# Half of V in loads of four heads, and wq issued ahead of x, in a cached-attention block

## The chip, the cores and the metric

The kernel runs on one core of one Trainium2 chip, in one launch. The metric is the device time of that core in microseconds (us): 235.49 us, the median of three runs from 235.37 to 235.5.

The engines that the text speaks of are TensorE (matrix products, PE in the profile, with its weight loads as PEld), VectorE (DVE), ScalarE (ACT), GpSimd (POOL) and SyncE (SP). SP does no arithmetic here; it issues nearly all the loads from memory.

## The reference

One decode step of a transformer block for a batch of two, all in float32. `c` gives six modulation vectors; the normalized and modulated `x` is projected to 32 query heads, which attend over the last 4096 positions of a cache with 8 key/value heads; `wo` projects back; a second normalized half is an MLP of width 1792.

```python
mod = (silu(c) @ w_mod).reshape(2, 6, 1, 512)
sa, ca, ga, sb, cb, gb = (mod[:, i] for i in range(6))
h = layernorm(x) * (1 + ca) + sa
x = x + ga * attention(h, k_cache, v_cache, wq, wo)   # window of 4096, 4 query heads per kv head
h = layernorm(x) * (1 + cb) + sb
x = x + gb * (silu(h @ w1) @ w2)
```

The cache window is most of the data: 2 batches x 8 heads x 4096 positions x 128 values, 32 MB for K and 32 MB for V. `w_mod` is 6 MB, `wq` and `wo` 8 MB each, `w1` and `w2` 3.5 MB each.

## The kernel before

**The ring.** All large loads go through `slots`, a ring of eight slots of 4096 floats per partition (`stream`, L70). `load_pair` (L77) takes two slots for the K or V of two heads of one batch (4 MB, 32 KB per partition); `load_runs` (L88) takes what a weight needs. A load waits until what stood in its slots has been read. All of these loads are issued by SP in program order, so a load that waits holds up those behind it. `w_mod` takes slots 0 to 2, `wq` slots 4 to 7.

**The start.** `w_mod`, `x` and `wq` are issued by SP (L105, L113, L114), the four small pieces of `c` by ScalarE (L109). `c` goes through the silu (`cT`, `scT`); 32 products make the modulation in `m_a` and `m_sp` (L259, L262). After those of k = 0 the program has the statistics of `x` (`moments`, L219: two small products, L227 and L235, and a square root). `h_a`, `hq_T` (L271 to L273) and the 32 products of `q` (L290) follow. Instructions outside the order kept by hand are placed by a planner, by when it thinks their inputs ready; those wrapped in `inorder` keep the program's order on their engine. `place` (L300) turns a half of `q` and copies it into `qbd`, the weights of the score products; `place(0)` stands ahead of the loop, `place(1)` in step 2.

**The loop.** There are eight steps, each for two heads of one batch. `fetch(s + 1)` issues K of the next step, then V of this one. `keys` transposes K on VectorE in eight pieces (L349), `scores` multiplies (L362), `maxima` and `exponentials` make the probabilities `pr`. `turn` (L403) transposes them (`xp`), spreads them (`zp`), runs four products (`pT`) and two ScalarE copies (L423) into `ptb`, the weights for V. `weighted` (L430) runs 16 products of 512 columns per step against V and copies the result out; `collect` (L448) adds the copy into `o_all` with four small products. In step s the loop transposes and scores K of s, and does `turn` and `weighted` of step s - 1.

**The end.** `wo`, `w1` and `w2` follow V in the ring; the projection, the MLP and the output close the kernel.

Of the kernel before, what the change touches and what calls it, by code (L numbers as in the profile page):

```python
# [23 lines left out]
def adaln_block(  # L24
# [45 lines left out]
    def stream(n=1):  # L70
# [3 lines left out]
        turn_of[0] = i + n  # L74
        return slots[:, i % RING : i % RING + n, :].rearrange("p s e -> p (s e)")

    def load_pair(cache, s):  # L77


        i, b = divmod(s, B)  # L80
        t = stream(2)
        nc.sync.dma_start(
            t,
            cache[b, 2 * i : 2 * i + 2, SK - W :, :].rearrange("e (u n) d -> u e (n d)", u=P // 2),
        )
        return t

    def load_runs(w, per, lo, hi):  # L88
# [18 lines left out]
    for b in range(B):  # L107
        for lo in (0, 2):
# [39 lines left out]
        id16[:, :, None].to_broadcast([P, 16, 2]),  # L148
        half[:, None, :].to_broadcast([P, 16, 2]),
    )  # L150
    odd = const([P, 2], "odd")
    nc.vector.tensor_reduce(
        odd, ident.rearrange("p (a r) -> p r a", r=2), axis=AX.X, op=ALU.add
# [15 lines left out]
    nc.gpsimd.tensor_copy(  # L169
        selh[:, :, 2 * HQ - 8 : 2 * HQ].rearrange("p m (e g) -> p m e g", e=2),  # L170
        id4.rearrange("p (e m g) -> p m e g", e=2, g=G),
    )

    quad = const([P, 4, P], "quad")
# [20 lines left out]
    for t in mrow:  # L195
        nc.gpsimd.memset(t, 0.0)

    ptb = [const([P, 16, 2, 16], f"ptb{i}") for i in range(2)]
# [6 lines left out]
    oTn = const([P, 32, 32], "oTn")  # L205
    nc.gpsimd.memset(oTn, 0.0)
    mod_sp = const([P, 4, P], "mod_sp")
    x1 = const([P, P], "x1")

# [124 lines left out]
    kt, vt, wot, kT = {}, {}, [], {}  # L334
    s_ps, pr, o_ps, o_sb = {}, {}, {}, {}

    def fetch(s):
# [16 lines left out]
    def scores(s, j):  # L354

        if j == 0:
            s_ps[s] = bank("A", f"s{s}")
        i, b = divmod(s, B)
        for c in range(2):
            for e in range(2):  # L360
                r, h = 64 * e + 32 * c, 2 * i + e
                inorder(nc.tensor.matmul(  # L362
                    s_ps[s][r : r + 32, :],
                    qbd[h // 4][:, h % 4, b, j, :],
                    kT[s, j][:, 32 * c : 32 * c + 32, e:32:2],
                    start=(j == 0),
                    stop=(j == 3),
                ))
# [17 lines left out]
        ))  # L386

    def exponentials(s):
        bp = bank("B", f"bp{s}")
# [4 lines left out]
        inorder(nc.scalar.activation(  # L394
            pr[s].rearrange("p t k -> p (t k)"),
            s_ps[s],
            AF.Exp,
            bias=bias,
            scale=SCALE,
            accum_out=rowsum[:, s : s + 1],  # L400
        ))

    def turn(s):  # L403

        xp = once.tile([P, 16, 32], F32, tag="xp", name=f"xp{s}")
        inorder(nc.vector.transpose(xp, pr[s]))  # L406
        zp = once.tile([P, 4, 16, 16], F32, tag="zp", name=f"zp{s}")
        inorder(nc.vector.tensor_mul(  # L408
            zp,
            xp[:, None, :, 0:16].to_broadcast([P, 4, 16, 16]),  # L410
            quarter[:, :, None, None].to_broadcast([P, 4, 16, 16]),
        ))
        tp = bank("C", f"pT{s}")[:, : 2 * P]
        for i in range(4):
            inorder(nc.tensor.matmul(  # L415
                tp[32 * i : 32 * i + 32, :],
                mix.rearrange("p v e -> p (v e)"),
                zp.rearrange("p y t x -> p (y t) x")[:, :, 4 * i : 4 * i + 4],
                start=True,
                stop=True,  # L420
            ))
        for e in range(2):
            inorder(nc.scalar.activation(  # L423
                ptb[s % 2][:, :, e, :],
                tp.rearrange("p (w z) -> p w z", z=16),
                AF.Copy,
                scale=odd[:, e : e + 1],
            ))

    def weighted(s):  # L430
# [14 lines left out]
        o_sb[s] = once.tile([P, 4 * DH], F32, tag="wide", name=f"ob{s}")  # L445
        inorder(nc.scalar.copy(o_sb[s], o_ps[s]))  # L446

    def collect(s):  # L448

        i, b = divmod(s, B)  # L450
        lo = 2 * HQ - 8 - (HQ * b + 2 * G * i)
        for m in range(4):
            r = 64 * (m % 2)
# [4 lines left out]
                start=(s == 0 and m < 2),  # L458
                stop=(s == STEPS - 1 and m >= 2),
                skip_group_check=True,  # L460
            ))
# [264 lines left out]
```

## Time and profile before

| what | value |
|---|---|
| median of the runs | 235.49 us |
| the profiled execution, span from first to last instruction | 233.6 us |
| median less span | 1.9 us |
| bytes moved by DMA | 97.68 MB, mean 418 GB/s |
| TensorE busy | 160.1 us (69%) |
| VectorE busy | 114.8 us (49%) |
| ScalarE, GpSimd busy | 28.9 us (12%), 10.5 us (5%) |
| mean granted TensorE clock | 0.927 |

In the profile, a row of the timeline has the start in us, the duration, the engine, the line of the kernel, the operation, the tiles (written <- read), their shapes and a count; at its end, in brackets, stands the idle time of the engine ahead of it and what ended that idle time. "SPq" and "ACTq" rows are issues of loads. Several instructions of one kind are merged into one row. A row of the stretches has the stretch and its length, the busy time and count of PE, PEld, DVE, ACT and POOL, the granted TensorE clock, the share of the DMA engines and GB/s. A row of DMA issues ends with the us from issue to landing. In rows of one tile's instructions stand the least, median and greatest duration in ns.

### The profile page before, as it was taken

Reading aid. Unit: us, or ns where it says so; the run is one execution under the profiler, and the core shown is the slowest. Engines: PE = TensorE matmul, PEld = TensorE weight load, DVE = VectorE, ACT = ScalarE, POOL = GpSimd, SP = SyncE. Lnnn points to the kernel's source line nnn. Section 1 sums busy time; section 2 is a strip of 40 time slices with the busy share of each in tenths; the row PEclk is TensorE's granted clock in tenths of the full one; section 3 lists DMA queues with packets and bytes.
Section 4 is the critical chain, followed back from the end, with each engine's and each line's share of the span. In section 5 each row is a group of like instructions: output and inputs, shape, how many; then the busy total and the mean of one; then the engine's idle time right before and its main releaser. Section 6 shows DMA issues by size and latency. Waiting matters only on the chain.

```text
span 233.6 us, 2565 instructions
## 1 busy us (share of the span) xinstructions
PE 160.1 (69%) x1070; PEld 42.0 (18%) x1070; DVE 114.8 (49%) x171; ACT 28.9 (12%) x65; POOL 10.5 (5%) x35
## 2 busy tenths in 40 slices
PE   0004806949687839787679759759769778789784
PEld 0001301201111111211111201201111122324222
DVE  3004310278794758696197179249559540101232
ACT  1100300000311120120210201111030030102020
POOL 8600000000000000000000000000000000000000
PEclk9999965988799976999999979997999997999999
DMA  7998998999999999999999999999999999989991
GB/s 269 438 551 359 393 505 359 440 449 415 415 432 449 436 438 415 421 438 446 443 426 415 424 443 449 438 421 421 424 450 438 443 407 463 463 351 439 425 409 66
DMA packets 3794, 97.68 MB, mean 418 GB/s; under 512 B 432, under 2 KB 456, under 8 KB 968
## 3 DMA queue, kind: packets, MB, share of 16 engines
q1 hardware_dynamic: 3768, 97.53, 97.2%
q8 instruction: 8, 0.13, 0.2%
q14 instruction: 2, 0.02, 0.0%
q10 hardware_dynamic: 16, 0.00, 0.0%
HBM read 97.53 MB, written 0.00 MB: 418 GB/s over the span
## 4 chain that ended last, share of the span: by engine, by line
DMA 60%; issue 18%; DVE 14%; PE 6%; POOL 1%; SPq 0%; POOLq 0%; ACT 0%; DVEq 0%
DMA slots<-in_A_k_cache_dram 22%; DMA slots<-in_A_wq_dram 14%; DMA slots<-in_A_v_cache_dram 12%; DMA slots<-in_B_w_dram 12%; DVE kT L349 11%; PE o L436 2%; PE q L290 2%; DVE zp L408 1%; PE acc_yw L655 1%; DVE xp L406 1%; PE acc_y L665 0%; DVE xc L102 0%; DVE qT L303 0%; POOL qg L307 0%; PE acc_y L546 0%
## 5 line engine op out<-in xcount | busy, mean ns | idle before, releaser
L349 DVE STREAM_TRANSPOSE kT<-slots 128x1024 f32<-128x1024 f32 x64 | 73.7, 1210 | 23.6 <-DMA slots<-in_A_k_cache_dram 23.6
L362 PE MATMUL s<-kT,qbd 128*32 128x512 f32 x256 | 70.5, 703 | 18.9 <-DVE kT L349 17.9
L436 PE MATMUL o<-slots,ptb 128*32 128x512 f32 x256 | 30.8, 624 | 2.1 <-DMA slots<-in_A_v_cache_dram 2.1
L362 PEld LDWEIGHTS s<-kT,qbd 128*32 128x32 f32 x256 | 9.9, 114 | 69.5 <-DVE kT L349 65.1
L259 PE MATMUL m_a<-slots,scT 128*32 128x256 f32 x32 | 2.9, 446 | 20.5 <-DVE scT L251 20.5
L290 PE MATMUL q<-slots,hq_T 128*32 128x512 f32 x64 | 8.7, 707 | 9.0 <-DMA slots<-in_A_wq_dram 9.0
L436 PEld LDWEIGHTS o<-slots,ptb 128*32 128x32 f32 x256 | 8.1, 113 | 17.9 <-issue 17.8
L392 ACT COPY bias<-bp 128x1 f32<-128x1 f32 x8 | 1.3, 159 | 77.1 <-PE bp L390 77.1
L372 DVE TENSOR_REDUCE mx<-s 128x1 f32<-128x512 f32 x8 | 5.5, 692 | 9.5 <-PE s L362 9.5
L559 PE MATMUL junk<-quad,id 128*32 128x512 f32 x22 | 10.2, 595 | 0.0
L408 DVE TENSOR_TENSOR zp<-xp,quarter 128x1024 f32<-128x1024 f32 x8 | 9.8, 1225 | 0.2
L423 ACT ACTIVATE ptb<-pT,odd 128x256 f32<-128x256 f32 x16 | 6.7, 473 | 25.7 <-PE pT L415 25.7
L303 DVE STREAM_TRANSPOSE qT<-q 128x512 f32<-128x512 f32 x2 | 1.4, 718 | 14.2 <-PE q L290 12.7
L446 ACT COPY ob<-o 128x512 f32<-128x512 f32 x8 | 4.7, 586 | 25.9 <-PE o L436 25.9
L415 PE MATMUL pT<-zp,mix 128*32 128x256 f32 x64 | 5.5, 416 | 3.0 <-DVE zp L408 2.9
L374 PE MATMUL mT<-ident,mx 128*1 128x128 f32 x16 | 3.0, 271 | 6.3 <-DVE mx L372 6.3
L406 DVE STREAM_TRANSPOSE xp<-pr 128x512 f32<-128x512 f32 x8 | 5.5, 685 | 3.6 <-ACT pr L394 3.6
L245 DVE STREAM_TRANSPOSE cT<-xc 128x128 f32<-128x128 f32 x1 | 0.4, 403 | 13.9 <-DMA xc<-in_c_dram 13.9
L573 PE MATMUL acc_o<-slots,oTn 128*32 128x512 f32 x56 | 6.2, 593 | 0.9 <-DMA slots<-in_A_wo_dram 0.9
L544 DVE COPY acc_o_sb<-acc_o 128x256 f32<-128x256 f32 x1 | 0.4, 424 | 12.7 <-ACT acc_o_sb L543 12.7
L390 PE MATMUL bp<-negscale,mrow 1*128 1x1 f32 x16 | 3.0, 254 | 4.3 <-DVE mrow L383 4.3
L454 PE MATMUL o_all<-ob,selh 128*64 128x128 f32 x64 | 5.3, 285 | 0.8 <-ACT ob L446 0.8
(136 smaller groups left out, 92.7 us busy)
## 6 DMA issues: line engine op xcount, KB each, us to landing
slots<-in_A_k_cache_dram SPq DMA_DIRECT2D x8, 4096.0 KB, 27.7
slots<-in_A_v_cache_dram SPq DMA_DIRECT2D x8, 4096.0 KB, 27.7
slots<-in_w_mod_dram SPq DMA_DIRECT2D x1, 6144.0 KB, 17.1
slots<-in_A_wo_dram SPq DMA_DIRECT2D x1, 6144.0 KB
slots<-in_B_w_dram SPq DMA_DIRECT2D x1, 2688.0 KB
slots<-in_A_wo_dram SPq DMA_DIRECT2D x1, 2048.0 KB, 29.5
slots<-in_B_w_dram SPq DMA_DIRECT2D x1, 2048.0 KB
slots<-in_B_w_dram SPq DMA_DIRECT2D x1, 896.0 KB
```

The lines of the kernel that those rows point to most:

```text
L290: nc.tensor.matmul(q_ps[n][32 * g : 32 * g + 32, :], hq_T[:, k, :], wv[:, n, g], start=(k == 0), stop=(k == 3),)
L349: inorder(nc.vector.transpose(kT[s, j][:, 32 * c : 32 * c + 32, :], kt[s].rearrange("p (n j r) -> p j n r", j=4, r=32)[:, j, 32 * c : 32 * ...
L362: inorder(nc.tensor.matmul(s_ps[s][r : r + 32, :], qbd[h // 4][:, h % 4, b, j, :], kT[s, j][:, 32 * c : 32 * c + 32, e:32:2], start=(j == ...
L372: inorder(nc.vector.tensor_reduce(mx, s_ps[s], axis=AX.X, op=ALU.max))
L406: inorder(nc.vector.transpose(xp, pr[s]))
L408: inorder(nc.vector.tensor_mul(zp, xp[:, None, :, 0:16].to_broadcast([P, 4, 16, 16]), quarter[:, :, None, None].to_broadcast([P, 4, 16, 16 ...
L415: inorder(nc.tensor.matmul(tp[32 * i : 32 * i + 32, :], mix.rearrange("p v e -> p (v e)"), zp.rearrange("p y t x -> p (y t) x")[:, :, 4 * ...
L423: inorder(nc.scalar.activation(ptb[s % 2][:, :, e, :], tp.rearrange("p (w z) -> p w z", z=16), AF.Copy, scale=odd[:, e : e + 1],))
L436: inorder(nc.tensor.matmul(o_ps[s][r : r + 32, :], ptb[s % 2][:, w].rearrange("p e z -> p (e z)"), vt[s].rearrange("p (c w m f d) -> p c f ...
L454: inorder(nc.tensor.matmul(o_all[r : r + 64, :], selh[:, m, lo : lo + 2 * HQ], o_sb[s][:, m * DH : (m + 1) * DH], start=(s == 0 and m < 2) ...
L559: inorder(nc.tensor.matmul(junk[0:32, :], id4, quad.rearrange("p m y -> p (m y)"), start=True, stop=True,))
L573: inorder(nc.tensor.matmul(acc[32 * g : 32 * g + 32, :], oTn[:, q, :], wot[q], start=(q < 4), stop=(q >= 24),))
```

## The change

V of steps 0 to 3 comes in two loads, each of four heads of one batch (8 MB, 64 KB per partition, slots 4 to 7). V of steps 4 to 7 stays in loads of two heads. `spot` gives the new order of the steps: steps 0 and 1 are the first four heads of batch 0, steps 2 and 3 those of batch 1, then the last four heads of each in the same way. For a pair of steps, `turn` writes the weights of both into one tile `ptq` (eight small products per step instead of four, and wider ScalarE copies, with the new constants `mixq` and `fourth`), and `weighted_four` runs 64 products of 256 columns and two collecting products (with the new constant `selb`), at the start of steps 2 and 4. `turn` of steps 1 and 3 moves to the end of its own step, ahead of the first transposes of the next. `oTn` now shares memory with the second half of `ptq` and is cleared in step 4.

`wq` is issued ahead of `x`, and `x` in three loads of four, two and two rows.

```diff
+    def spot(s):
+        return s // (2 * B) * 2 + s % 2, s // 2 % B
+
     def load_pair(cache, s):
-        i, b = divmod(s, B)
+        i, b = spot(s)
...
+    def load_four(cache, p):
+        t = stream(4)
+        inorder(nc.sync.dma_start(
+            t,
+            cache[p % B, p // B * 4 : p // B * 4 + 4, SK - W :, :].rearrange(
+                "e (u n) d -> u e (n d)", u=P // 4
+            ),
+        ))
+        return t
...
-    nc.sync.dma_start(rows8(x_sp), x2.rearrange("b (g m) -> g b m", m=P))
     wqt = load_runs(wq, 4, 0, 4)
+    for b, lo, hi in ((0, 0, 4), (1, 0, 2), (1, 2, 4)):
+        nc.sync.dma_start(
+            x_sp.rearrange("(g y) m -> g y m", g=4)[lo:hi, 16 * b, :],
+            x2[b].rearrange("(g m) -> g m", m=P)[lo:hi],
+        )
...
     def fetch(s):
         if s < STEPS:
             kt[s] = load_pair(k_cache, s)
-        if s > 0:
+        if s % 2 and s // 2 < BIG:
+            vb[s // 2] = load_four(v_cache, s // 2)
+        elif s > 2 * BIG:
             vt[s - 1] = load_pair(v_cache, s - 1)
...
+        if s < 2 * BIG:
+            tq = bank("C", f"pT{s}")
+            for q in range(2):
+                for i in range(4):
+                    inorder(nc.tensor.matmul(
+                        tq[32 * i : 32 * i + 32, 2 * P * q : 2 * P * q + 2 * P],
+                        mixq[:, s % 2, q].rearrange("p u b e -> p (u b e)"),
+                        zp.rearrange("p y t x -> p (y t) x")[:, :, 4 * i : 4 * i + 4],
+                        start=True,
+                        stop=True,
+                    ))
+            for e in range(2):
+                h = s % 2 * 2 + e
+                inorder(nc.scalar.activation(
+                    ptq[:, :, h, :],
+                    tq.rearrange("p (w z) -> p w z", z=8),
+                    AF.Copy,
+                    scale=fourth[:, h : h + 1],
+                ))
+            return
...
+    def weighted_four(p):
+        o_ps[p] = bank("D", f"oq{p}")[:, : 2 * DH]
+        v = vb[p].rearrange("p (q c t m f d) -> p q c f t m d", q=2, c=2, t=8, m=2, f=2)
+        for w in range(64):
+            r = 32 * (w % 4)
+            inorder(nc.tensor.matmul(
+                o_ps[p][r : r + 32, :],
+                ptq[:, w].rearrange("p h z -> p (h z)"),
+                v[:, w // 32, w // 16 % 2, w // 8 % 2, w % 8],
+                start=(w < 4),
+                stop=(w >= 60),
+            ))
+        ob = once.tile([P, 4 * DH], F32, tag="wide", name=f"obq{p}")[:, : 2 * DH]
+        inorder(nc.scalar.copy(ob, o_ps[p]))
...
     for s in range(STEPS + 1):
+        big = s < 2 * BIG
+        if s in (2, 4):
+            weighted_four(s // 2 - 1)
+        if s == 2 * BIG:
+            nc.gpsimd.memset(oTn, 0.0)
         if s < STEPS:
             fetch(s + 1)
             scores(s, 0)
-        if s > 0 and s != STEPS - 1:
+        if big and s % 2 or s > 2 * BIG and s != STEPS - 1:
             turn(s - 1)
-        if s > 1:
+        if s > 2 * BIG + 1:
             collect(s - 2)
...
+        if big and s % 2:
+            turn(s)
         if s < STEPS - 2:
             keys(s + 1, 0)
-        if s > 0:
+        if s > 2 * BIG:
             weighted(s - 1)
```

More of the change, by code (lines that the diff above doesn't have):

```diff
@@ L150, in adaln_block @@
     )
+    mixq = const([P, 2, 2, 8, 2, 2], "mixq")
+    nc.gpsimd.memset(mixq, 0.0)
+    for b in range(B):
+        for q in range(2):
+            nc.gpsimd.tensor_mul(
+                mixq[:, b, q, :, b, :],
+                id16[:, q:16:2][:, :, None].to_broadcast([P, 8, 2]),
+                half[:, None, :].to_broadcast([P, 8, 2]),
+            )
+    fourth = const([P, 4], "fourth")
+    nc.vector.tensor_reduce(
+        fourth, ident.rearrange("p (a r) -> p r a", r=4), axis=AX.X, op=ALU.add
+    )
     odd = const([P, 2], "odd")
@@ L446, in weighted @@
         inorder(nc.scalar.copy(o_sb[s], o_ps[s]))
+    def weighted_four(p):
[9 more added lines that the diff above has]
+                stop=(w >= 60),
+            ))
+        ob = once.tile([P, 4 * DH], F32, tag="wide", name=f"obq{p}")[:, : 2 * DH]
+        inorder(nc.scalar.copy(ob, o_ps[p]))
+        lo = 32 - (p % B * HQ + p // B * 16)
+        for m in range(2):
+            inorder(nc.tensor.matmul(
+                o_all[64 * m : 64 * m + 64, :],
+                selb[:, m, lo : lo + 64],
+                ob[:, m * DH : (m + 1) * DH],
+                start=(p == 0),
+                stop=False,
+                skip_group_check=True,
+            ))
     def collect(s):
-        i, b = divmod(s, B)
+        i, b = spot(s)
         lo = 2 * HQ - 8 - (HQ * b + 2 * G * i)
@@ L457, in collect @@
                 o_sb[s][:, m * DH : (m + 1) * DH],
-                start=(s == 0 and m < 2),
+                start=False,
                 stop=(s == STEPS - 1 and m >= 2),
```

28 lines of the change are left out of this document (21 added, 7 removed).

## The prediction

> **What bounds the kernel now.** I read the page first, for the share of the DMA queue, then the timeline of the vector engine for the moments at which K landed, then the timeline of SP, which issues every load.
>
> ```profile
> span 233.6 us, 2565 instructions
> ...
> PEclk9999965988799976999999979997999997999999
> ...
> q1 hardware_dynamic: 3768, 97.53, 97.2%
> ...
> slots<-in_w_mod_dram SPq DMA_DIRECT2D x1, 6144.0 KB, 17.1
> ```
>
> The queue of SP is busy for 97.2% of the span of 16 engines. No engine is the limit, then. Does it ever run dry between its first and its last load? The first transposes of the K of steps 3, 4 and 6, each of which waited for its load, say no:
>
> ```profile
> 96.73 2.37 DVE L349 STREAM_TRANSPOSE kT<-slots 128x1024 f32<-128x1024 f32 x2 [1.16 <-DMA slots<-in_A_k_cache_dram]
> 116.03 2.37 DVE L349 STREAM_TRANSPOSE kT<-slots 128x1024 f32<-128x1024 f32 x2 [5.50 <-DMA slots<-in_A_k_cache_dram]
> 154.76 2.37 DVE L349 STREAM_TRANSPOSE kT<-slots 128x1024 f32<-128x1024 f32 x2 [5.49 <-DMA slots<-in_A_k_cache_dram]
> ```
>
> Two 4 MB loads (V, then K) lie between the first two rows: 19.30 us, 9.65 each. Four lie between the last two: 38.73 us, 9.68 each. The pace is constant, and each load is issued well before it can start. So the end moves only if the rate changes or if the queue runs dry. Everything else is a matter of slack.
>
> **The change part by part.** *Descriptors of 64 KB in place of 32 KB for half of V.* wq already has rows of 65536 bytes per partition:
>
> ```profile
> 0.73 0.38 SPq L93 DMA_DIRECT2D slots<-in_w_mod_dram  x1
> ...
> 3.32 0.61 SPq L93 DMA_DIRECT2D slots<-in_A_wq_dram  x1
> 27.03 1.83 SPq L82 DMA_DIRECT2D slots<-in_A_k_cache_dram  x2
> 44.34 0.54 SPq L82 DMA_DIRECT2D slots<-in_A_v_cache_dram  x1
> 46.06 0.54 SPq L82 DMA_DIRECT2D slots<-in_A_k_cache_dram  x1
> ```
> ```profile
> slots<-in_A_wq_dram SPq DMA_DIRECT2D x1, 33.8
> ```
>
> w_mod landed at 0.73 + 17.1 = 17.8, wq at 3.32 + 33.8 = 37.1: 19.3 us for 8 MB, as much as two pairs take. Two such loads gain nothing to 0.15 us (2 x the 0.06 us between 2 x 9.68 and 19.3, and rounding). I take -0.1.
>
> *Two fewer V issues, two more x issues.* SP issues a load in 0.38 to 0.61 us and otherwise waits; the sum of issues is the same. SP is not on the path: cost 0, covered by the transfers under way.
>
> *x behind wq.* A queue serves its loads in order: in the rows above K of step 0 is issued at 27.03 and follows wq. So x, 4 KB, now lands with wq at about 37.2, not with w_mod. What follows x:
>
> ```profile
> 20.41 0.29 DVE L222 BATCH_NORM_STATS2 st_a<-xc 128x6 f32<-128x128 f32 x1
> 23.26 0.54 PE L227 MATMUL mean_a<-mv_a,avg 128*128 128x1 f32 x2
> 27.47 0.29 DVE L271 SCALAR_TENSOR_TENSOR h_a<-m_a,xn_a 128x128 f32<-128x128 f32 x1 [0.56 <-PE m_a L259]
> 28.12 0.40 DVE L245 STREAM_TRANSPOSE hq_T<-h_a 128x128 f32<-128x128 f32 x1
> ...
> 37.26 8.32 PE L290 MATMUL q<-slots,hq_T 128*32 128x512 f32 x60 [9.00 <-DMA slots<-in_A_wq_dram]
> ...
> 47.06 0.29 DVE L317 COPY qbd<-qr 32x128 f32<-32x128 f32 x1 [0.32 <-ACT qbd L317]
> 48.48 9.13 DVE L349 STREAM_TRANSPOSE kT<-slots 128x1024 f32<-128x1024 f32 x8 [1.13 <-DMA slots<-in_A_k_cache_dram]
> ```
>
> From the first mean product to the end of hq_T it is 28.52 - 23.26 = 5.26 us, less the 0.56 us that h_a waited for m_a, plus about 0.6 for the statistics: 5.3 us. Today they end at 28.5 and q waits for wq alone. Then q starts at 42.5 instead of 37.26 and is 5.3 us late. The issue that waits for all of wq (46.06) becomes 51.4, and now it is the 8 MB V load, which needs all four slots. K of step 0 landed at 48.46, so K of step 1 drains near 58.1; a load issued at 51.4 is in time by some 5 us. The price here is therefore slack, not time. It is paid further on: the copies into qbd end at 47.35 + 5.3 = 52.7, they stand ahead of the first key transposes on the vector engine, so step 0 starts 4.2 us later (52.7 against 48.48).
>
> c, on a queue of its own, has landed by 17.91 (the row of cT below); its last rows may now stand behind one descriptor of wq, 19.3 / 8 = 2.4 us. That puts the K issue of 27.03 at 29.5, against 36: covered.
>
> I also assume that the tensor engine runs the m_a and m_sp products of all four k before the two mean products. Today they alternate (23.26 stands inside them), and the two loads at 27.03 wait for the last of them. The order is a planner's; today it put the x statistics behind the whole chain of c, as if x came late, so with x later I expect the mean products behind. The other case is rival B.
>
> *Weights of two steps turned and spread over 64 rather than 2 x 16 products.* The pattern that repeats, with its durations:
>
> ```profile
> 58.80 0.69 DVE L372 TENSOR_REDUCE mx<-s 128x1 f32<-128x512 f32 x1 [1.20 <-PE s L362]
> ...
> 63.14 0.71 DVE L406 STREAM_TRANSPOSE xp<-pr 128x512 f32<-128x512 f32 x1 [0.47 <-ACT pr L394]
> 63.89 1.23 DVE L408 TENSOR_TENSOR zp<-xp,quarter 128x1024 f32<-128x1024 f32 x1
> ...
> 65.26 0.64 PE L415 MATMUL pT<-zp,mix 128*32 128x256 f32 x8 [0.62 <-DVE zp L408]
> 65.96 0.84 ACT L423 ACTIVATE ptb<-pT,odd 128x256 f32<-128x256 f32 x2 [2.85 <-PE pT L415]
> ...
> 73.09 0.69 DVE L372 TENSOR_REDUCE mx<-s 128x1 f32<-128x512 f32 x1 [1.19 <-PE s L362]
> ...
> 75.11 3.64 PE L436 MATMUL o<-slots,ptb 128*32 128x512 f32 x32
> 75.41 0.69 ACT L394 ACTIVATE pr<-s,bias 128x512 f32<-128x512 f32 x1
> ...
> 76.00 0.19 ACT L394 ACTIVATION_READ_ACCUMULATOR pr<-s,bias 128x1 f32 x1
> ```
> ```profile
> L436 PE MATMUL o<-slots,ptb x256: 589/592/1061, 75.1 to 198.3; 128*32 128x512 f32 x128
> L259 PE MATMUL m_a<-slots,scT x32: 379/379/634, 20.5 to 27.0; 128*32 128x256 f32 x32
> ```
>
> From mx to the weights for V: probabilities ready 76.19 - 73.09 = 3.1; transpose and zp 63.14 to 65.12, 2.0; twice the pT products, 1.3; two ScalarE copies of 512 columns, by the pr row 0.69 each at most and by the 0.84 row at least 0.84 in all, I take 1.3. Together 7.7 us. The four-head product: 64 calls of 256 columns carry as many columns as two of today's (3.64 each), 7.3 us with each one's start-up. If a 256-column call kept the ratio of the single durations (379 to 592), it would be 4 x 3.64 x 0.64 = 9.3. I take 7.0 to 7.3, since the products are pipelined and follow their columns.
>
> Now the two places where the 8 MB buffer can starve the queue. **Second V load**: the mx of step 1 moves from 73.09 to 77.3; weights at 85.0; the product ends at 92.2; then SP issues. It must be issued before K of step 3 has drained, which lands at 96.7 as now. The first bytes follow an issue by about 1.2 us (below, the issue at 0.73), so the limit is near 95.2: slack 3.0.
>
> ```profile
> 0.00:1.00 1.00, 0.00 (x0) 0.00 (x0) 0.00 (x0) 0.00 (x0) 0.47 (x6) 1.00 0.00 0
> 1.00:2.00 1.00, 0.00 (x0) 0.00 (x0) 0.21 (x1) 0.00 (x0) 0.92 (x3) 1.00 1.63 492
> ```
>
> **V of step 4** waits only for the first half of the second product (two of its four slots; so today the issue at 44.34 waited for the half of wq it overwrites and not for the rest):
>
> ```profile
> 83.09 0.72 DVE L303 STREAM_TRANSPOSE qT<-q 128x512 f32<-128x512 f32 x1 [1.49 <-PE o_all L454]
> ...
> 85.91 6.88 DVE L349 STREAM_TRANSPOSE kT<-slots 128x1024 f32<-128x1024 f32 x6
> ...
> 93.98 0.69 DVE L372 TENSOR_REDUCE mx<-s 128x1 f32<-128x512 f32 x1 [1.19 <-PE s L362]
> ```
>
> Placing the second half of q shares its buffer with the four-head result, so it now starts some 1.1 us after the first product (copy out, two collecting products): 93.3. From there to the mx of step 2 it is 10.9 as in these rows: 104.2. From mx to mx 14.3 (58.80 to 73.09): 118.5. Weights 7.7 later, 126.2, half a product 3.6: issue at 129.8. K of step 5 drains at 135.4 (two loads before the 154.76 row); less 1.2 the limit is 134.2: slack 4.4. The loads between (K of 4 and 5) need steps 2 and 3 transposed, at about 103 and 117, against limits near 114 and 124. From step 4 on loads, slots and products are today's, with the vector engine up to 7 us late; a step costs it some 14 us of 19.3, so it catches up before the last loads.
>
> *Constants.* Five more GpSimd products and memsets for mixq, two for selb, one reduction on the vector engine: about 0.2 to 0.35 us each, in a stretch where both idle.
>
> ```profile
> 17.91 0.40 DVE L245 STREAM_TRANSPOSE cT<-xc 128x128 f32<-128x128 f32 x1 [13.95 <-DMA xc<-in_c_dram]
> 29.00 0.53 POOL L275 TENSOR_SCALAR mod_sp<-mod_sp 128x128 f32<-128x128 f32 x1 [19.56 <-ACT mod_sp L274]
> ```
>
> They are hidden by those 13.95 and 19.56 us; uncovered they would be 1.5 us. The clearing of oTn moves into step 4 and is wanted only after the last V.
>
> **Sum**: 233.6 - 0.1 + 0 + 0 = 233.5 of span; the median of the runs is 1.9 above the span, so **235.4 us**, no change that can be told: a measurement of this kernel tells about 0.2%, 0.5 us.
>
> **Rivals.** *A, the product runs cold (slower).* The place is the two four-head products, behind a pause of the tensor engine while the weights are turned (77 to 85). The granted clock fell to half after such a pause:
>
> ```profile
> 84.00:88.00 4.00, 1.27 (x4) 0.49 (x6) 2.87 (x6) 0.52 (x2) 0.37 (x2) 0.63 0.97 418
> 88.00:92.00 4.00, 4.00 (x18) 0.75 (x16) 4.00 (x5) 0.00 (x0) 0.00 (x0) 0.52 0.95 410
> ```
>
> About 7 us of half clock there. A spell of that length would cost the first product 3.4 and the half of the second 3.6: 7.0 against a slack of 4.4, so 2.6 us of empty queue. With the 9.3 us product as well, 3.4 more. It decides from 4.4 us on. Typical spells in the page's PEclk row are one slice of 5.8 us at 0.5 to 0.7, worth 1.5 to 2 us each, 3 to 4 in all: just under. Price 2 us in the middle: **237.5**. By the Trainium skill (TensorE: Matmul & The Clock Gate, "What's actually happening") the clock is set over free-running windows of 3.4 us, half after an idle one; one cold window at each product would cost 3.4 in all and no time, two at the first one 5.1 and 0.7 us. The 0.63 and 0.52 rows agree with the halving; they do not show the window.
>
> *B, the mean products keep their place.* They would wait for x with the rest of m_a behind them; the two K loads would be issued at 37.2 + 0.6 + 27.03 - 23.26 = 41.6, first bytes at 42.8, with the queue empty since 37.1: 5.7 us, **241.1**. Against it: the planner's order above.
>
> *C, fewer and longer loads are faster.* K of step 0 landed 11.3 us after wq, 1.7 over the pace; were that the price of a boundary between loads, two boundaries fewer would give 3.4 us, **232.1**. Against it: 9.65 to 9.68 at all later boundaries. The Trainium skill (DMA: Bandwidth & Descriptors, "Anatomy of one DMA") has about 2 us fixed for each transfer on another issuing path, which for two loads would be 4 us; the constant pace shows that queued loads here don't pay it.
>
> *D, x is not late* (the rows of x slip in as those of c do, whose queue is another). Then all slacks grow by 4.2 and the time is the forecast's.
>
> **How the numbers follow.** Forecast 54%, D 8%: both no change. A 22%, B 9%: slower. C 7%: faster. The likeliest time is 235.4, by itself 235.1 to 235.9. The range, 235.0 to 238.6, leaves out B, C and the far end of A. Faster 0.07, same 0.62, slower 0.31.
>
> **What would show it.** q starting near 42.5 and the first key transposes near 52.7 show x late; 37.3 shows D. The K loads issued near 27 to 30 speak against B, near 41 for it. The second V load should be issued at 92 to 95 and that of step 4 at 130 to 134; later than 95 or 134, with K of step 6 landing after 154.8, is A. Landings of K of steps 3, 4, 5 and 6 at today's times within 0.3 us confirm the forecast. It is wrong if the DMA row shows a gap, or if 8 MB of V take other than 19.3 us.

## The result and the profile after

The changed kernel takes 241.82 us (median of five runs, 240.76 to 242.43) against 235.37 us for the kernel before on the same chip (235.33 to 235.5). The ratio is 1.0264, 95% interval 1.0244 to 1.0285: 6.4 us slower. The prediction said 235.4, with a range up to 238.6. The profiled run took 240.76 us, of which its span is 238.6: 5.0 us more span than before, and 2.2 us outside it, against 1.9.

First the page of the changed kernel, the same rows as of before and the shares of the chain that ended last:

```profile
span 238.6 us, 2841 instructions
...
PEclk9999975599979758978895699999999999997999
...
q1 hardware_dynamic: 3484, 97.53, 95.7%
...
DMA 39%; PE 38%; DVE 16%; ACT 4%; issue 2%; POOL 0%; DVEq 0%; ACTq 0%
```

The bytes are the same, and the queue of SP is busy for 95.7% of a longer span instead of 97.2%. In the chain, TensorE has 38%. The same row of the kernel before:

```profile
DMA 60%; issue 18%; DVE 14%; PE 6%; POOL 1%; SPq 0%; POOLq 0%; ACT 0%; DVEq 0%
```

So somewhere loads now wait for TensorE. The timeline of SP after shows which:

```profile
28.51 1.85 SPq L86 DMA_DIRECT2D slots<-in_A_k_cache_dram  x2
...
95.87 0.54 SPq L95 DMA_DIRECT2D slots<-in_A_v_cache_dram  x1
...
136.38 0.54 SPq L86 DMA_DIRECT2D slots<-in_A_v_cache_dram  x1
```

The two issues that the prediction watched came at 95.87 (second V load, predicted 92.2) and 136.38 (V of step 4, predicted 129.8). What the queue did around them, in rows of stretches of the changed kernel (the last two columns are the share of the 16 DMA engines and GB/s; a row counts a packet, with all its bytes and all its time, where the packet begins, so that a share can be over 1 and a low one says that few packets began):

```profile
94.00:95.00 1.00, 1.00 (x28) 0.52 (x24) 0.00 (x0) 0.00 (x0) 0.00 (x0) 1.00 0.14 49
95.00:96.00 1.00, 0.80 (x16) 0.22 (x8) 0.00 (x0) 0.07 (x1) 0.00 (x0) 1.00 0.15 66
96.00:97.00 1.00, 0.65 (x8) 0.35 (x12) 0.09 (x1) 0.30 (x1) 0.00 (x0) 1.00 0.00 0
97.00:98.00 1.00, 0.83 (x8) 0.00 (x0) 0.95 (x3) 0.00 (x0) 0.27 (x2) 1.00 2.68 852
...
136.00:137.00 1.00, 1.00 (x25) 0.52 (x20) 1.00 (x2) 0.00 (x0) 0.00 (x0) 1.00 0.31 131
```

From 94 to 97 almost no packet begins, and at 136 there are few again. The timeline of VectorE says what that cost, by the landings of K that the transposes waited for:

```profile
37.37 0.29 DVE L266 BATCH_NORM_STATS2 st_a<-xc 128x6 f32<-128x128 f32 x1 [5.92 <-DMA xc<-in_A_x_dram]
...
53.31 9.13 DVE L398 STREAM_TRANSPOSE kT<-slots 128x1024 f32<-128x1024 f32 x8
...
77.93 0.69 DVE L421 TENSOR_REDUCE mx<-s 128x1 f32<-128x512 f32 x1 [1.20 <-PE s L411]
...
121.50 0.69 DVE L421 TENSOR_REDUCE mx<-s 128x1 f32<-128x512 f32 x1 [1.20 <-PE s L411]
...
128.23 9.13 DVE L398 STREAM_TRANSPOSE kT<-slots 128x1024 f32<-128x1024 f32 x8 [1.63 <-DMA slots<-in_A_k_cache_dram]
...
179.04 9.13 DVE L398 STREAM_TRANSPOSE kT<-slots 128x1024 f32<-128x1024 f32 x8 [2.01 <-DMA slots<-in_A_k_cache_dram]
```

The landing of K of step 7 is the measure for all that follows. It stands behind the same bytes in both kernels, and before it came at:

```profile
174.16 9.13 DVE L349 STREAM_TRANSPOSE kT<-slots 128x1024 f32<-128x1024 f32 x8 [1.95 <-DMA slots<-in_A_k_cache_dram]
```

So it is 4.9 us late, which is the growth of the span (5.0). K of step 4 has one pair more ahead of it than before; at the constant pace it would land at 116.03 + 9.67 = 125.7, and it landed at 128.23. So by these landings about 2.5 us were lost at the second V load, and the rest, 2.2 to 2.4, at V of step 4. A landing tells of the slowest of the 16 DMA engines alone. The single packets, whose times the trace keeps though no view prints them, give the mean: around the second V load an engine stood idle for 2.6 us, and its packets took 0.7 us more than usual (1.21 us for 32 KB, 2.42 us for 64 KB); around V of step 4 it was 0.8 and 0.6. That is 3.4 and 1.4 us, 4.8 together.

What made the issues late stands in the timeline of TensorE and in the granted clock of the changed kernel:

```profile
43.19 8.75 PE L334 MATMUL q<-slots,hq_T 128*32 128x512 f32 x64 [3.36 <-DVE hq_T L289]
...
83.18 1.93 PE L467 MATMUL pT<-zp,mixq 128*32 128x256 f32 x16 [3.16 <-DVE zp L458]
86.49 9.31 PE L524 MATMUL oq<-slots,ptq 128*32 128x256 f32 x128 [1.38 <-ACT ptq L476]
...
130.06 9.71 PE L524 MATMUL oq<-slots,ptq 128*32 128x256 f32 x128 [1.38 <-ACT ptq L476]
```
```profile
80.00:82.00 2.00, 0.02 (x1) 0.00 (x0) 0.91 (x2) 0.94 (x3) 0.00 (x0) 0.69 0.95 410
82.00:84.00 2.00, 0.82 (x8) 0.45 (x12) 1.03 (x1) 0.00 (x0) 0.00 (x0) 0.50 1.14 492
84.00:86.00 2.00, 1.11 (x12) 0.23 (x4) 0.00 (x0) 0.83 (x2) 0.00 (x0) 0.50 0.88 377
86.00:88.00 2.00, 1.51 (x16) 0.78 (x20) 0.96 (x1) 0.43 (x1) 0.00 (x0) 0.50 1.02 434
88.00:90.00 2.00, 2.00 (x24) 0.87 (x20) 1.42 (x2) 0.00 (x0) 0.00 (x0) 0.50 1.11 475
90.00:92.00 2.00, 2.00 (x36) 1.01 (x32) 0.00 (x0) 0.00 (x0) 0.00 (x0) 0.75 0.83 360
```

The clock was at half while the weights were turned and for the first half of the product. Both four-head products took over 9 us instead of the 7.0 to 7.3 forecast.

### The profile page after: what moved, and what is told of

Read it like the earlier page. It is cut to its first block, busy times and chain, and to the rows that moved or that the text cites. A ratio compares the mean times of both kernels' runs of the same rounds, so it can differ in the third digit from the quotient of the medians.

```text
span 238.6 us, 2841 instructions
## 1 busy us (share of the span) xinstructions
PE 159.6 (67%) x1206; PEld 47.9 (20%) x1206; DVE 115.5 (48%) x172; ACT 28.9 (12%) x63; POOL 11.8 (5%) x42
## 3 DMA queue, kind: packets, MB, share of 16 engines
q1 hardware_dynamic: 3484, 97.53, 95.7%
## 4 chain that ended last, share of the span: by engine, by line
DMA 39%; PE 38%; DVE 16%; ACT 4%; issue 2%; POOL 0%; DVEq 0%; ACTq 0%
PE s L411 17%; DMA slots<-in_B_w_dram 12%; DMA slots<-in_A_v_cache_dram 12%; DMA xc<-in_A_x_dram 8%; PE oq L524 8%; DMA slots<-in_w_mod_dram 7%; DVE kT L398 7%; PE q L334 4%; PE pT L467 3%; DVE zp L458 3%; DVE mx L421 2%; PE o L506 2%; DVE xp L456 1%; ACT ptq L476 1%; ACT pr L444 1%
## 5 line engine op out<-in xcount | busy, mean ns | idle before, releaser
L411 PE MATMUL s<-kT,qbd 128*32 128x512 f32 x256 | 63.3, 657 | 10.7 <-DVE kT L398 9.7
L524 PE MATMUL oq<-slots,ptq 128*32 128x256 f32 x256 | 19.0, 469 | 2.8 <-ACT ptq L476 2.8
L411 PEld LDWEIGHTS s<-kT,qbd 128*32 128x32 f32 x256 | 9.2, 110 | 53.6 <-DVE kT L398 47.8
L506 PE MATMUL o<-slots,ptq 128*32 128x512 f32 x128 | 14.6, 595 | 2.4 <-DMA slots<-in_A_v_cache_dram 2.4
L524 PEld LDWEIGHTS oq<-slots,ptq 128*32 128x32 f32 x256 | 9.2, 134 | 13.4 <-issue 5.1
L467 PE MATMUL pT<-zp,mixq 128*32 128x256 f32 x64 | 6.8, 561 | 7.0 <-DVE zp L458 6.9
L662 PE MATMUL junk<-quad,id 128*32 128x512 f32 x22 | 10.2, 595 | 0.0
L676 PE MATMUL acc_o<-slots,ptq 128*32 128x512 f32 x56 | 7.9, 727 | 2.5 <-DMA slots<-in_A_wo_dram 2.5
L476 ACT ACTIVATE ptq<-pT,fourth 128x512 f32<-128x512 f32 x8 | 5.1, 684 | 16.3 <-PE pT L467 16.3
L271 PE MATMUL mean_a<-mv_a,avg 128*128 128x1 f32 x2 | 0.6, 348 | 8.4 <-DVE mv_a L268 8.4
L303 PEld LDWEIGHTS m_a<-slots,scT 128*32 128x32 f32 x32 | 1.1, 135 | 25.2 <-DVE scT L295 22.7
```

What stands on the lines that cost most here:

```text
L411: inorder(nc.tensor.matmul(s_ps[s][r : r + 32, :], qbd[h // 4][:, h % 4, b, j, :], kT[s, j][:, 32 * c : 32 * c + 32, e:32:2], start=(j == ...
L467: inorder(nc.tensor.matmul(tq[32 * i : 32 * i + 32, 2 * P * q : 2 * P * q + 2 * P], mixq[:, s % 2, q].rearrange("p u b e -> p (u b e)"), z ...
L476: inorder(nc.scalar.activation(ptq[:, :, h, :], tq.rearrange("p (w z) -> p w z", z=8), AF.Copy, scale=fourth[:, h : h + 1],))
L506: inorder(nc.tensor.matmul(o_ps[s][r : r + 32, :], ptb[s % 2][:, w].rearrange("p e z -> p (e z)"), vt[s].rearrange("p (c w m f d) -> p c f ...
L524: inorder(nc.tensor.matmul(o_ps[p][r : r + 32, :], ptq[:, w].rearrange("p h z -> p (h z)"), v[:, w // 32, w // 16 % 2, w // 8 % 2, w % 8], ...
L662: inorder(nc.tensor.matmul(junk[0:32, :], id4, quad.rearrange("p m y -> p (m y)"), start=True, stop=True,))
```

## The experiments

The theory after the first look: the loss is a missed deadline at two places, and three things bring it about: x late by some 5 us, a cold TensorE clock, and a deadline that lies earlier than the prediction put it. The rivals: long loads are slow in themselves; the late x costs time wherever it stands; the gaps at the two places are separate prices that add.

**x ahead of wq again, the rest of the change kept.**

```diff
-    wqt = load_runs(wq, 4, 0, 4)
-    for b, lo, hi in ((0, 0, 4), (1, 0, 2), (1, 2, 4)):
-        nc.sync.dma_start(
-            x_sp.rearrange("(g y) m -> g y m", g=4)[lo:hi, 16 * b, :],
-            x2[b].rearrange("(g m) -> g m", m=P)[lo:hi],
-        )
+    nc.sync.dma_start(rows8(x_sp), x2.rearrange("b (g m) -> g b m", m=P))
+    wqt = load_runs(wq, 4, 0, 4)
```

> The changed kernel with x in one load ahead of wq again; the four-head V loads stay. Theory (the 8 MB buffer is read out too late, and 4.8 us of that lateness is x landing behind wq): x lands near 18, the product q starts near 37.3, the second V load is issued at 90 to 93 and that of step 4 at 130 to 133, and the queue hardly empties: 235.3 to 236.5 us. Rival 1 (the 8 MB loads themselves cost it, wherever x stands): within 1 us of 241.8.

Measured: 237.16 us (235.95 to 239.42), ratio 1.0073 (1.0026 to 1.0121). 4.7 of the 6.4 us came back, which is less than the theory had and far from rival 1. The issues and the landings of K of steps 4 and 7, from the timelines of SP and VectorE of this kernel:

```profile
90.43 0.54 SPq L95 DMA_DIRECT2D slots<-in_A_v_cache_dram  x1
...
130.78 0.54 SPq L86 DMA_DIRECT2D slots<-in_A_v_cache_dram  x1
```
```profile
125.57 9.13 DVE L394 STREAM_TRANSPOSE kT<-slots 128x1024 f32<-128x1024 f32 x8 [4.41 <-DMA slots<-in_A_k_cache_dram]
...
174.98 9.13 DVE L394 STREAM_TRANSPOSE kT<-slots 128x1024 f32<-128x1024 f32 x8 [2.11 <-DMA slots<-in_A_k_cache_dram]
```

Both issues are 5.4 to 5.6 us earlier. The second V load costs nothing now: K of step 4 is at its nominal 125.7. V of step 4, issued at 130.78, 3.4 us inside the limit that the prediction gave (134.2), still cost 0.8 us. So that limit was wrong by itself.

**The late x alone, in the kernel before.**

```diff
-    nc.sync.dma_start(rows8(x_sp), x2.rearrange("b (g m) -> g b m", m=P))
     wqt = load_runs(wq, 4, 0, 4)
+    for b, lo, hi in ((0, 0, 4), (1, 0, 2), (1, 2, 4)):
+        nc.sync.dma_start(
+            x_sp.rearrange("(g y) m -> g y m", g=4)[lo:hi, 16 * b, :],
+            x2[b].rearrange("(g m) -> g m", m=P)[lo:hi],
+        )
```

> The kernel before with wq issued ahead of x and x in three loads, V in pairs throughout. Theory: q starts near 43, step 0 some 5 us late, but a pair load never waits for two steps, so the queue stays full: 235.2 to 235.9 us. Rival 2 (x behind wq costs its 5 us by itself): 240 us or more.

Measured: 236.14 us, ratio 1.003 (1.0017 to 1.0043). K of step 7 and the product of the first w2 load come when they came before (174.16 and 226.42), or a trace earlier:

```profile
174.09 9.13 DVE L353 STREAM_TRANSPOSE kT<-slots 128x1024 f32<-128x1024 f32 x8 [1.92 <-DMA slots<-in_A_k_cache_dram]
...
226.34 1.92 PE L659 MATMUL acc_yw<-slots,uT 128*32 128x512 f32 x16 [0.74 <-DMA slots<-in_B_w_dram]
```

With pairs, the 5 us of lateness are swallowed by slack. The time is 0.2 us above the range of the theory and far below the rival's. Of the 0.8 us that x behind wq did cost, 0.2 lie in the span (233.8) and some 0.25 outside it in the profiled run (235.95 us); why is not known.

**The clock kept up.** Ten products of 512 columns whose result nobody reads, in TensorE's idle time of steps 1 and 3.

```diff
         inorder(nc.vector.tensor_reduce(mx, s_ps[s], axis=AX.X, op=ALU.max))
+        if s in (1, 3):
+            warm("C", 1, f"wa{s}")
...
+        if s in (1, 3):
+            warm("C", 3, f"wb{s}")
         bias = work.tile([P, 1], F32, tag="bias", name=f"bias{s}")
...
+            if s % 2:
+                warm("A", 1, f"wc{s}")
             for e in range(2):
```

> The changed kernel with five idle-time products added in each of steps 1 and 3 while the weights are turned, their results unused, so that the tensor engine's clock stays up. Theory: the turning products take 1.1 instead of 1.9 us and the four-head product 7 instead of 9.3 to 9.7; the second V load is issued near 93, that of step 4 near 130 to 131: 235.4 to 236.8 us. Rival (the cold clock is a detail; the buffer frees too late anyway): over 239.

Measured: 237.54 us (236.83 to 239.4), ratio 1.0102 (1.007 to 1.0135). 4.3 us came back, so the clock is no detail, but the time is 0.7 us above the range of the theory. The rows of SP, VectorE and TensorE of this kernel:

```profile
52.81 0.54 SPq L95 DMA_DIRECT2D slots<-in_A_v_cache_dram  x1
...
93.55 0.54 SPq L95 DMA_DIRECT2D slots<-in_A_v_cache_dram  x1
...
130.55 0.54 SPq L86 DMA_DIRECT2D slots<-in_A_v_cache_dram  x1
```
```profile
78.75 0.69 DVE L421 TENSOR_REDUCE mx<-s 128x1 f32<-128x512 f32 x1 [1.21 <-PE wa L461]
...
87.27 2.37 DVE L398 STREAM_TRANSPOSE kT<-slots 128x1024 f32<-128x1024 f32 x2 [3.48 <-DMA slots<-in_A_k_cache_dram]
...
127.97 9.13 DVE L398 STREAM_TRANSPOSE kT<-slots 128x1024 f32<-128x1024 f32 x8 [3.74 <-DMA slots<-in_A_k_cache_dram]
...
176.37 9.13 DVE L398 STREAM_TRANSPOSE kT<-slots 128x1024 f32<-128x1024 f32 x8 [2.09 <-DMA slots<-in_A_k_cache_dram]
```
```profile
86.38 7.11 PE L538 MATMUL oq<-slots,ptq 128*32 128x256 f32 x128 [0.56 <-ACT ptq L490]
```

This run grants the prediction its clock. From mx to the product it is 7.63 us (7.7 forecast), and the product takes 7.11 (7.0 to 7.3 forecast). The second V load goes out at 93.55, well inside the limit of 95.2, and yet K of step 4 lands 2.3 us after its 125.7. Not all of that belongs to the second V load: the keys of step 0 start 0.8 us later here than in the change (54.12), the first V load went out at 52.81, 5.0 us ahead of the landing of K of step 1 (57.8), and K of step 2 was already 0.5 us late (87.27, against 86.77 with x ahead and a warm clock, below). V of step 4, at 130.55, then costs nothing more: K of step 7 follows K of step 4 by 48.40 us, five loads of 9.68.

**Each 8 MB load as two 4 MB loads of half the slots**, so that the first half may start when half the product has been read.

```diff
-        inorder(nc.sync.dma_start(
-            t,
-            cache[p % B, p // B * 4 : p // B * 4 + 4, SK - W :, :].rearrange(
-                "e (u n) d -> u e (n d)", u=P // 4
-            ),
-        ))
+        src = cache[p % B, p // B * 4 : p // B * 4 + 4, SK - W :, :].rearrange(
+            "e (u n) d -> u e (n d)", u=P // 4
+        )
+        for lo in (0, 8192):
+            inorder(nc.sync.dma_start(t[:, lo : lo + 8192], src[:, :, lo : lo + 8192]))
```

> The changed kernel with each 8 MB V load issued as two loads of two slots in the same layout, so that the first half of the second V waits for half of the first product only. Theory (the last absolute deadline decides): the first half is issued near 92 and the queue no longer empties there, but V of step 4 is still issued near 136, so the whole loss moves to that place: 241 to 242 us. Rival 3 (the two gaps add up): the first gap's 2.5 us come back, 239.3 us.

Measured: 242.03 us (241.1 to 242.38), ratio 1.0279 (1.0257 to 1.0301): nothing came back. The issues and the stretches around the second of them:

```profile
93.39 3.99 SPq L99 DMA_DIRECT2D slots<-in_A_v_cache_dram  x2
137.51 0.54 SPq L86 DMA_DIRECT2D slots<-in_A_v_cache_dram  x1
```
```profile
134.00:135.00 1.00, 1.00 (x16) 0.53 (x12) 1.00 (x2) 0.00 (x0) 0.00 (x0) 0.50 0.23 98
135.00:136.00 1.00, 1.00 (x16) 0.46 (x12) 1.00 (x2) 0.00 (x0) 0.00 (x0) 0.50 0.00 0
...
137.00:138.00 1.00, 1.00 (x27) 0.57 (x20) 0.00 (x0) 0.00 (x0) 0.00 (x0) 1.00 0.00 0
```

The first gap is nearly filled (by the single packets an engine lost 0.7 us there on average, in place of 3.4), and the queue then stands empty for four us at the second (4.8 us lost, in place of 1.4). The rival that the gaps are separate prices falls. The moment at which V of step 4 can be issued is set by the chain of TensorE and VectorE, which did not get shorter (the second product starts at 131.03, in the change at 130.06); whatever is saved at the first place is paid at the second.

**x ahead and the clock kept up together**, the edits of the first and the third experiment.

> x ahead of wq again and the idle-time products, with the 8 MB loads. Theory (lateness of reading out the buffer is all of it, and a load must be issued some 3 us before the queue drains): the second V load is issued near 88, that of step 4 near 126, both over 5 us before the drain near 94.7 and 133.4: 235.3 to 236.0 us. Rival (something else of the 8 MB loads costs the 1.8 us that stayed with x ahead): 236.8 us or more.

Measured: 236.92 us (236.68 to 237.06), ratio 1.0064 (1.0049 to 1.0079). The issues, from the timeline of SP, and the landings of K:

```profile
87.64 0.54 SPq L95 DMA_DIRECT2D slots<-in_A_v_cache_dram  x1
124.97 0.54 SPq L86 DMA_DIRECT2D slots<-in_A_v_cache_dram  x1
```
```profile
86.77 2.37 DVE L394 STREAM_TRANSPOSE kT<-slots 128x1024 f32<-128x1024 f32 x2 [8.89 <-DMA slots<-in_A_k_cache_dram]
125.51 9.13 DVE L394 STREAM_TRANSPOSE kT<-slots 128x1024 f32<-128x1024 f32 x8 [6.85 <-DMA slots<-in_A_k_cache_dram]
...
174.15 9.13 DVE L394 STREAM_TRANSPOSE kT<-slots 128x1024 f32<-128x1024 f32 x8 [2.41 <-DMA slots<-in_A_k_cache_dram]
```

K of step 7 is where it was before the change, to 0.01 us: the 4.9 us are gone to the last. From K of step 2 to K of step 4 it is 38.74 us for 16 MB, the 8 MB load among them: four times 9.68, the old pace. Yet the kernel is 1.4 us slower than before, as the rival had it, and this part is another matter (below).

**One 8 MB load only, x ahead** (BIG = 1; V of steps 2 and 3 in pairs again).

> x ahead of wq, one 8 MB load (V of steps 0 and 1) and pairs from step 2 on, no idle-time products. Theory: V of step 2 needs half of the one four-head product, issued near 87 against a drain near 94.7, and no second product follows: 235.3 to 236.2 us. Rival (each 8 MB load costs by itself): half of the 1.8 us with two, 236.3 us or more.

Measured: 235.67 us, ratio 1.0013 (1.0003 to 1.0023). No gain from the longer rows, and next to no loss where the one deadline is kept (V of step 2 was issued at 88.09).

**The two remaining pairs of edits**: the halves and the warm clock with x late, and the same with x ahead.

> x still behind wq; idle-time products, and each 8 MB load in two halves. Theory: V of step 4 issued near 130.5 as with the idle-time products alone, and the first half of the second V at 90, 4.5 us before the drain: no place left where the queue empties, 235.6 to 236.5 us, the last part what x behind wq costs with pairs. Rival (halving never matters, the products added cost the rest): 237.5 us, as without the halves.

> All three: x ahead of wq, idle-time products, halves. Theory: the queue has all the slack that it had before, and longer descriptors are no faster: 235.2 to 235.8 us, no better than the kernel before. Rival (four-head buffers are worth something once they starve nothing): under 235.

Measured: 237.32 us, ratio 1.0084 (1.0069 to 1.0099), and 236.86 us, ratio 1.0055 (1.0038 to 1.0072), both about a us above the ranges of their theories. K of step 7 landed at 174.54 and 174.19. The queue's loss is thus nearly gone in the one and wholly in the other; what is left is the same remainder of 1.3 to 1.5 us as with x ahead and a warm clock.

**The remainder.** In the three variants that keep the clock up and meet the deadlines, K of step 7 is within 0.4 us of its old time and the end is not. (The warm variant with x late is not among them: in its profiled run K of step 7 was 2.2 us late, and the span 3.7 us longer.) The first w2 load of the variant with x ahead and a warm clock lands late, and that of before, in the second fence, does not:

```profile
208.05 7.91 PE L686 MATMUL acc_o<-slots,ptq 128*32 128x512 f32 x56 [2.53 <-DMA slots<-in_A_wo_dram]
...
227.56 1.92 PE L768 MATMUL acc_yw<-slots,uT 128*32 128x512 f32 x16 [1.62 <-DMA slots<-in_B_w_dram]
```
```profile
226.42 1.92 PE L655 MATMUL acc_yw<-slots,uT 128*32 128x512 f32 x16 [0.75 <-DMA slots<-in_B_w_dram]
```

Four runs asked what it hangs on. The place of the code in memory was the first suspect: 14 and 32 one-column products with an unread result at the start of the kernel before, and 50 in the variant with x ahead and a warm clock, each to shift all code behind them.

```diff
+    idle = bank("C", "idle")
+    for _ in range(14):   # 32, 50
+        nc.tensor.matmul(idle[0:32, 0:1], id4, id4[:, 0:1], start=True, stop=True)
```

> The kernel before with 14 one-column products (56 TensorE instructions with their weight loads, results unused) at the start, where TensorE idles until 20 us. Theory of the last 1.2 us (TensorE's code comes in blocks of 256 instructions by the same 16 DMA engines; where a block is fetched among the last loads, the engine that fetches it is last): the last block, fetched at 229.2 now, comes near 223 and the last load of w2 lands about 1 us later: 236.2 to 237.0 us. Rival (the blocks are too small to matter): 235.2 to 235.7 us.

> The kernel before with 32 one-column products (128 instructions, half a block) at the start. Theory: the blocks are fetched half a block earlier, so one falls near 215 to 220, ahead of the last loads, and the time is within 0.7 us of 235.4, better or worse by which DMA engine fetches it. Rival: 235.4 to 235.6 us whatever is put there.

> x ahead of wq, idle-time products, 8 MB loads, and 50 one-column products (200 instructions) at the start, which puts TensorE's last instructions at the same place of a block of 256 as in the kernel before. Theory: the last block is fetched after the last load again, the 1.2 us come back: 235.3 to 236.0 us. Rival (the 8 MB loads or the added products cost the 1.4 us): 236.8 us or more.

Measured: 235.35, 235.39 and 237.12 us, ratios 0.9996 (0.9987 to 1.0006), 0.9995 (0.9985 to 1.0005) and 1.0064 (1.0043 to 1.0085). Shifting the code brought no loss to the one kernel and took none from the other: as put, the suspicion falls. In the padded variant the loss showed in the second load of wo already, for which the last products waited until 214.03; so the place of the slip moved with the code, though not its size.

Then the added products themselves, ten of them in the kernel before:

```diff
         inorder(nc.vector.tensor_reduce(mx, s_ps[s], axis=AX.X, op=ALU.max))
+        if s in (1, 3):
+            warm("C", 5, f"wa{s}")
```

> The kernel before, with five products of 128 x 512 columns whose result nobody reads put into the idle time of TensorE behind the row maxima of steps 1 and 3 (ten in all; in the variants that keep TensorE warm the same ten are spread over the same stretch of these steps). No load of 8 MB, x ahead of wq. The residue of 1.4 us (0.6%) that is left in the warm variants with two 8 MB loads and x ahead is either (a) the price of the added products, whatever the loads are: then this kernel takes 236.8 us, 0.6% more than before; or (b) it comes with the two 8 MB loads and their late readers: then this kernel takes the time of before, 235.4 us, within 0.2%. The queue should be full to the end in both cases.

Measured: 235.38 us, ratio 1.0 (0.9991 to 1.0009). They cost nothing. In this run's trace the projection by wo ran as cold as in the variant with x ahead and a warm clock (7.91 us, 6.21 in the kernel before), and the product of the first w2 load still started in time:

```profile
208.10 7.91 PE L583 MATMUL acc_o<-slots,oTn 128*32 128x512 f32 x56 [2.59 <-DMA slots<-in_A_wo_dram]
...
226.34 1.92 PE L665 MATMUL acc_yw<-slots,uT 128*32 128x512 f32 x16 [0.29 <-DMA slots<-in_B_w_dram]
```

So neither the products nor the cold projection are the cause. The remainder comes with the two four-head loads or the code that serves them, shows as a late landing of one of the last weight loads, and no run shows its cause.

The single packets of the traces bring the suspicion back in a narrower form. The queue that the page calls "q8 instruction" brings code in packets of 16 KB, which hold one DMA engine for some 0.9 us. In the variant with x ahead and a warm clock such a packet ran from 223.1 to 224.1. Until then the last engine was 0.75 us behind the median of the 16, and in the next landing, that of the first w2 load, one engine was 1.98 us behind; the other 15 had finished by 226.17, it at 227.42. In all six profiles that show the loss (x ahead, warm, and the four with both or with the halves and a warm clock) a single engine falls back in this way, by 1.0 to 1.6 us, in the landing that follows such a packet, in the padded one after 212.0, and in none of the other eight does one. The added products of the first padded run did move the packet as expected, from 229.2 to 223.1, but without a loss, and the kernel before with ten added products has one at 223.4 without a loss too. What would differ is how far back the engine stood that had to fetch. No run chose the engine, so this is not shown.

Of the change's own 6.4 us, 4.9 are the queue's, and the other 1.5 are for the most part the 0.3 outside the span and 1.1 by which the median lies above the profiled run. No version beat the kernel before.

## Why the prediction was wrong

The two edits that could be undone alone make a square. K of step 7 is late against 174.16 by:

| | clock as it comes | clock kept up |
|---|---|---|
| x late | 4.9 us (241.82 us) | 2.2 us (237.54 us) |
| x ahead | 0.8 us (237.16 us) | 0.0 us (236.92 us) |

The lateness is that of one profiled run of each kernel. Those of x ahead and of the warm clock with x late took 1.6 and 1.9 us more than the medians in the table, that of the change 1.1 us less. Each edit alone returns more than half, and both together not their sum: the mark of a deadline, not of two prices.

**The step that failed: "so the limit is near 95.2: slack 3.0", and the 134.2 like it.** They came from the landing of the load in front less 1.2 us to the first bytes of an issue (96.7 less 1.2 is 95.5, where the prediction has 95.2; the difference decides nothing). The runs put issue and loss side by side. The load in front of the second V load is K of step 3, 9.67 us after K of step 2; the one in front of V of step 4 is K of step 5, 9.67 us after K of step 4. The fifth column is the loss of the next K that waited, counted from the K that waited before it: from step 2 to 4 against 38.74 us and from step 4 to 7 against 48.64, which is what the variant with x ahead and a warm clock took. The last column is the mean over the 16 engines, from the single packets.

| kernel | place | issued | ahead of the landing in front | loss of the next K | mean loss of an engine |
|---|---|---|---|---|---|
| x ahead, warm | V of step 4 | 124.97 | 10.2 | 0 | 0.0 |
| x ahead, warm | second V load | 87.64 | 8.8 | 0 | 0.0 |
| warm | V of step 4 | 130.55 | 7.1 | 0 | 0.0 |
| x ahead | second V load | 90.43 | 6.1 | 0 | 0.0 |
| warm | first V load | 52.81 | 5.0 | 0.5 | 0.6 |
| x ahead | V of step 4 | 130.78 | 4.4 | 0.8 | 0.8 |
| warm | second V load | 93.55 | 3.4 | 2.0 | 1.2 |
| the change | V of step 4 | 136.38 | 1.5 | 2.2 | 1.4 |
| the change | second V load | 95.87 | 0.8 | 2.5 | 3.4 |

An issue is in time 6 us ahead of that landing, and not at 5. The prediction took 1.2. As the time from an issue to its first packet that was right: after the issue at 95.87 the first packet began at 97.2, after that at 93.55 at 94.9. But two things come on top. A landing is when the last engine has finished: in the changed kernel the engines were done with K of step 3 from 94.6 to 96.7, half of them by 94.9. The queue is empty for the many well before the load counts as landed. The Trainium skill says what the prediction should have read with it (DMA: Bandwidth & Descriptors, "Why a DMA increments its semaphore by 16 and not by 1"): a transfer runs on up to 16 engines that finish independently, and only the full count means that all data has landed. Those 16 times agree. And a load that is issued late begins slowly: the first packets of the second V load took up to 3.8 us in the change and up to 4.1 us in the warm variant, where 2.42 us is usual. In the warm variant that is most of the 1.2 us, and idle engines are 0.3. Why they are slow, and why 5 us ahead is not yet enough, no run shows. With a limit near 91, the prediction's own 92.2 was late already.

**The clock, rival A.** Its mechanism was right, and the place and the sign. It was given 22% and 237.5 us, because its price was read from single slices of the page. At half clock the way from mx to the product was 8.56 us (86.49 less 77.93), and at full clock 7.63; the product was 9.31 against 7.11. That is 3.1 us at the second V load. The mx of step 3 carries the 3.0 on (121.50, forecast 118.5); the weights of its step take 0.9 more and half the product 2.7 (6.3 from 130.06 to 136.38, against 3.6). The sum of 6.6 is the lateness of V of step 4 against the forecast. The rival's pessimistic case, "7.0 against a slack of 4.4", had this size, and the prediction took the middle instead. By the Trainium skill (TensorE: Matmul & The Clock Gate, "What's actually happening") the clock is set over windows of 3.4 us. The six rows from 80 to 92 hold 10.2 us of half clock (twice the sum of each row's length times what it lacks to 1), which would be three such windows; the prediction worked out one and two.

**What held.** x lands with wq, so rival D fell: its statistics start at 37.37, q at 43.19 (forecast 42.5), the keys of step 0 at 53.31 (52.7). The two K loads were issued at 28.51, so the mean products stand behind all of m_a, and rival B fell. The weights, 7.7 us, and the product, 7.0 to 7.3, held wherever the clock was full. Rows of 64 KB keep the pace of 9.68 us for 4 MB, so rival C fell. The added constants are hidden: with them, but with no lateness, K of step 7 lands at 174.15. The 1.9 us outside the span became 2.2.

**What the prediction left out.** The slack of the late x, of the longer chain and of the clock is one and the same slack. The text tested x first ("slack, not time"), then the chain, then the clock as a rival, each against what the one before had left, with a bound for the clock but none for the limit. Even by its own numbers the clock's 3.4 us at the first product was more than the 3.0 left at the second V load; it held only the sum of both, 7.0, against the 4.4 at V of step 4. The limit was the number most in doubt, and it got no range.

## What to carry to other kernels

Where a queue is full, a change is worth what it does to the latest moment at which each issue may come. Put a range on that moment, take it well ahead of when the first engines run dry rather than from the landing (here 5 to 6 us ahead of the landing in front), and count every lateness upstream against one slack. Larger buffers that are released all at once turn a slack of many small loads into a few deadlines: the same late x cost 4.1 us of landing with the 8 MB loads as changed (4.9 less 0.8), 2.2 with a warm clock, and none with pairs. And when weights are prepared in a pause of TensorE, price the products after it at half clock.

## What the runs showed of the hardware

- A load's landing says little about when its queue is free: half of the 16 engines were through 1.8 us before it (94.9 against 96.7). An issue 6.1 us ahead of the landing in front cost nothing, one 5.0 us ahead cost 0.6 us for each engine.
- Inside that limit the price rises all the way: 0.8 us for each engine at 4.4 us ahead, 1.2 at 3.4, 1.4 at 1.5, 3.4 at 0.8. The next landing hides this (2.0 us late at 3.4, 2.5 at 0.8), because it tells of the slowest engine alone.
- A product that had begun did not lift the clock at once: TensorE was busy for 1.11 and 1.51 of 2 us in the rows from 84 to 88, and fully from 88, and the clock began to come back only in the row from 90 (0.75).
- Ten products of 512 columns with an unread result kept the clock up over two pauses: in the warm variant it is 1.00 in every row of 2 us from 76 to 92 and from 120 to 132. Ten of them in the kernel before, all behind the row maxima, cost nothing (235.38 against 235.37 us), though so placed they did not keep it up (0.50 from 86 to 92).
- Some kernels with two 8 MB loads lose 1.3 to 1.5 us in the landings of the last weight loads, with a full queue until then. In the profiles one of the 16 engines is late, right behind a 16 KB packet of code that held an engine for 0.9 us; that this is the cause is not shown.
